# The upper parts of the values of the later batches are written by VectorE instead of ScalarE

## The chip, the cores and the metric

One core of a Trainium2 chip runs the whole program. The metric is device time in microseconds (us); lower is better. Before the change, three runs gave a median of 1901.4 us (1901.28 to 1903.27). Below, TensorE does matrix products and loads their weights, VectorE, ScalarE and GpSimd do the work on elements, and SyncE issues the transfers.

## The reference, cut to what matters

Attention through 49 agents, on 4 batches of 12480 tokens of 128 channels, then a layer of two products with a squared ReLU between them.

```python
def _attn_ref(q, k, v, agents):
    scale = 1.0 / np.sqrt(q.shape[-1])
    def sm(a, b):
        s = scale * (a @ b.transpose(0, 2, 1))
        s = s - s.max(-1, keepdims=True)
        e = np.exp(s)
        return e / (e.sum(-1, keepdims=True) + 1e-09)
    a2k = sm(agents, k)          # B x 49 x 12480
    agent_v = a2k @ v            # B x 49 x 128
    q2a = sm(q, agents)          # B x 12480 x 49
    return (q2a @ agent_v).astype(np.float32)

def _moe_ref(x, w_in, w_out):    # x: 49920 x 128, w_in: 128 x 2048, w_out: 2048 x 128
    h = np.maximum(x @ w_in, 0.0)
    return (h * h @ w_out).astype(np.float32)
```

## The kernel before

Each batch is first boiled down to a table: `agent_v` times `w_in`, so that the first layer of a token is its 49 weights times that table. Tokens go in 13 blocks of 960 per batch, each in two halves of 480. A number is held as a rounded upper part (float32r) and the remainder, a lower part, so that each product is done from parts; the three groups of products of the second layer (`g_lo` with `wo_half`, `g_hi` with `wo_hi`, `g_hi` with `wo_lo`) are such.

The main loop has 416 steps, here called steps, of two chunks of 256 hidden units each. A step is `first` (lines 494 to 527) and `second` (546 to 563). In `first`, TensorE makes four products `h<-w,aw_hi` and adds four `h<-x,aw_ex`, into two of three PSUM buffers `h` (`ps_h`, two banks each). ScalarE writes `r` from each `h` and then `g_hi`, VectorE writes `gg` from the first `h`, then `h` in place and `g_lo` from the second; GpSimd writes the two other `g_lo` (line 519). With three buffers and two to a step, the third of a step's four weight loads `h<-w,aw_hi` goes into the buffer that the step before used first: it waits for that step's `gg`. `second` works on the chunks of two steps before and sums into `o`; every eighth chunk VectorE writes `ob` out of `o`.

Between these, two background streams run in the gaps: the next blocks' query weights (`queries`: on VectorE `m`, `e`, `z`, its reciprocal; on GpSimd `e`, `ph`, `y`, `half`), and the table of the next batch (`background`, from line 571). The latter first takes the scores of all 13 blocks of keys, then their maxima (`maxima`: `dg` on VectorE, the product with it on TensorE, `mb`), and then 13 units of values, one in about 17 us: `weighed` prepares a unit and `gathered` multiplies it and adds it to `av` on VectorE. The values of batch 0 take another path (`whole`), so the units below are those of batches 1, 2 and 3, 39 in all. "The first batch" below means the first one with such units.

In a unit, the tile `vs` holds for 120 tokens by 8 the upper parts of 128 values, a one, and the lower parts. Line 280 writes the upper parts, a copy that rounds; line 282 on GpSimd subtracts them from the values for the lower parts, and 278 and 279 set the rest.

Each engine works through its own queue in order. The matrix products and the main loop's operations are chained in the order in which they are written (`queued`, line 487); the place of the background work among them is chosen by the scheduler when the program is built, from its own estimates.

Of the kernel before, what the change touches and what calls it, by code (L numbers as in the profile page):

```python
# [41 lines left out]
def agent_attention_relu2(ctx: ExitStack, tc: tile.TileContext, qT, kT, v, agT, w_in, w_out, outT):  # L42
    nc = tc.nc
    C, NTOK = qT.shape
# [218 lines left out]
    def halves(out, x, n, eng):  # L263

        nc.scalar.copy(out[:, :, :n], x)
        yield PACE
        last[eng] = eng.tensor_sub(out[:, :, n:], x, out[:, :, :n].bitcast(F32))

    def weighed(b, i, vt, whole, eng):
        st = state[b]  # L270
        s = st["s"][i]
        mb = st["mb"].rearrange("p (o a) -> p o a", o=1).broadcast_to([TP, NT, NA])
        d = s if whole else small.tile([TP, NT, NA], F32, name="d", bufs=2)
        st["less"] = eng.tensor_sub(d, s, mb).ins
        R, W = (NA, C + 1) if whole else (K2, 2 * (C + 1))
        if not whole:
            vs = kv.tile([TP, NT, W], F32R, name="vs")
            nc.gpsimd.memset(vs.bitcast(F32)[:, :, C : C + 1], 1.0)
            nc.gpsimd.memset(vs.bitcast(F32)[:, :, 2 * C + 1 :], 0.0)
            nc.scalar.copy(vs[:, :, :C], vt[:, :, :C])  # L280
            yield PACE
            last[nc.gpsimd] = nc.gpsimd.tensor_sub(  # L282
                vs[:, :, C + 1 : 2 * C + 1], vt[:, :, :C], vs[:, :, :C].bitcast(F32)
            )
        else:
            nc.scalar.copy(vt[:, :, C:], ones[:TP, :NT].rearrange("p (t o) -> p t o", o=1))
        yield PACE
        nc.scalar.activation(d, d, AF.Exp, scale=scale)
        if whole:
            e = d  # L290
        else:
            e = small.tile([TP, NT, R], F32R, name="e2", bufs=2)
            yield from halves(e, d, NA, eng)
            vt = vs
        return e, vt, R, W, whole
# [28 lines left out]
    def values(b, i, vt, whole, eng):  # L324
        yield from gathered(b, i, *(yield from weighed(b, i, vt, whole, eng)))
# [245 lines left out]
    def background(b):  # L571

        kt = load_keys(b, 0, kv, "kt")
        for i in range(NB):
            nxt = load_keys(b, i + 1, kv, "kt") if i + 1 < NB else load_values(b, 0, kv, "vt")
            yield from scores(b, i, kt)
            yield 0.5
            kt = nxt
        yield from maxima(b)
        yield  # L580
        vt = load_values(b, 1, kv, "vt")
        ready = yield from weighed(b, 0, kt, False, nc.gpsimd)
        for i in range(NB):
            yield PACE
            nxt = load_values(b, i + 2, kv, "vt") if i + 2 < NB else None
            more = (yield from weighed(b, i + 1, vt, False, nc.gpsimd)) if i + 1 < NB else None
            yield from gathered(b, i, *ready)
            vt, ready = nxt, more
        yield
        yield from tables(b)  # L590
# [151 lines left out]
```

## Time and profile before

| what | value |
|---|---|
| median of 3 runs | 1901.4 us |
| profiled execution | 1903.08 us, its span 1900.9 us |
| TensorE busy | 1877.9 us (99%), chain that ended last: 89% TensorE |
| VectorE busy | 1648.2 us (87%) |
| ScalarE busy | 1670.7 us (88%) |
| GpSimd busy | 1335.3 us (70%) |
| granted TensorE clock, mean | 0.992 |
| the copies of line 280 | 39, 40.2 us on ScalarE |
| the lower parts of line 282 | 39, 85.8 us on GpSimd |

Four engines have long busy times, but a busy time is an average. The waits of TensorE, by what ended them, tell what a shorter or longer queue elsewhere would be worth.

### The profile page before, as it was taken

How to read it: one execution, taken by the hardware profiler on the slowest of the kernel's cores; microseconds unless marked ns; L12 is line 12 of the kernel's file. 1: busy time of each engine (PE TensorE's matmuls, PEld its weight loads, DVE VectorE, ACT ScalarE, POOL GpSimd, SP SyncE). 2: the span in 40 equal slices, each digit the busy share in tenths (PEclk: the TensorE clock that was granted, in tenths of full speed). 3: DMA queues.
4: the chain of work that ended last, by engine and by line, in shares of the span. 5: the costliest groups of instructions: out<-in, count | busy, mean ns of one | idle time of the engine just before them, and what ended most of it. 6: DMA issues, size and time to landing. Idle time of an engine off the chain costs nothing.

```text
span 1900.9 us, 31102 instructions
## 1 busy us (share of the span) xinstructions
PE 1877.9 (99%) x10848; PEld 1404.6 (74%) x10848; DVE 1648.2 (87%) x1918; ACT 1670.7 (88%) x1607; POOL 1335.3 (70%) x1270
## 2 busy tenths in 40 slices
PE   8899999999999999999999999999999999999999
PEld 8678777777678777777767777777767777777776
DVE  6887888888987888888998788888899989989897
ACT  4478899998888899999888789999889999999997
POOL 1455789887665589887666568989666676767675
PEclk9799999999999999999999999999999999999999
DMA  9233222221123222222112322222111111111110
GB/s 359 74 122 93 81 83 76 90 74 52 51 75 99 92 85 73 89 69 71 50 46 88 104 69 75 86 71 73 49 46 55 52 52 53 51 51 44 57 35 30
DMA packets 74148, 144.53 MB, mean 76 GB/s; under 512 B 9356, under 2 KB 45864, under 8 KB 73992
## 3 DMA queue, kind: packets, MB, share of 16 engines
q1 hardware_dynamic: 73992, 142.55, 23.6%
q8 instruction: 86, 1.41, 0.3%
q14 instruction: 70, 0.57, 0.1%
HBM read 82.89 MB, written 25.56 MB: 57 GB/s over the span
## 4 chain that ended last, share of the span: by engine, by line
PE 89%; DVE 6%; issue 2%; ACT 1%; POOL 1%; DMA 0%; POOLq 0%; SPq 0%; DVEq 0%; ACTq 0%
PE o L490 53%; PE h L490 24%; PE psa L490 10%; DVE gg L490 2%; PE psa L305 1%; DVE g_lo L490 1%; PE h L194 1%; POOL g_lo L519 1%; ACT r L490 1%; DVE h L490 1%; DVE aw_half L388 1%; ACT g_hi L490 0%; DVE ob L490 0%; PE h L612 0%; DVE rest L115 0%
## 5 line engine op out<-in xcount | busy, mean ns | idle before, releaser
L519 POOL TENSOR_TENSOR g_lo<-gg,g_hi 128x480 f16<-128x480 f32 x832 | 998.2, 1221 | 423.4 <-ACT g_hi L490 263.8
L490 ACT ACTIVATE r<-h 128x960 f32<-128x960 f32 x832 | 763.5, 967 | 118.4 <-PE h L490 60.9
L490 ACT ACTIVATE g_hi<-r 128x1920 fp32r<-128x1920 f32 x416 | 754.2, 1813 | 30.3 <-ACT r L490 0.7
L490 DVE TENSOR_TENSOR g_lo<-h,g_hi 128x960 f16<-128x960 f32 x416 | 479.4, 1153 | 126.2 <-ACT g_hi L490 94.1
L490 PE MATMUL o<-g_hi,wo_hi 128*128 128x480 f32 x1664 | 569.4, 423 | 0.0
L490 DVE TENSOR_TENSOR gg<-r,h 128x960 f32<-128x960 f32 x416 | 479.1, 1152 | 83.8 <-ACT r L490 78.5
L490 PE MATMUL o<-g_lo,wo_half 128*128 128x480 f16 x1664 | 517.2, 370 | 0.5 <-POOL g_lo L519 0.5
L490 PE MATMUL o<-g_hi,wo_lo 128*128 128x480 f32 x1664 | 496.1, 379 | 0.0
L490 DVE TENSOR_TENSOR h<-r,h 128x960 f32<-128x960 f32 x416 | 480.2, 1154 | 1.1
L490 PE MATMUL h<-w,aw_hi 128*128 128x480 f32 x1664 | 434.9, 382 | 7.5 <-DVE gg L490 4.0
L490 PEld LDWEIGHTS h<-w,aw_hi 128*128 128x128 f32 x1664 | 312.5, 189 | 63.7 <-DVE gg L490 10.9
L490 PEld LDWEIGHTS o<-g_hi,wo_hi 128*128 128x128 f32 x1664 | 314.9, 189 | 50.3 <-issue 0.8
L490 PEld LDWEIGHTS o<-g_hi,wo_lo 128*128 128x128 f32 x1664 | 312.5, 188 | 48.8
L490 PEld LDWEIGHTS <-wo_half 128*128 128x128 f16 x1664 | 171.9, 112 | 149.0 <-issue 96.7
L490 PE MATMUL h<-x,aw_ex 19*128 19x480 f16 x1664 | 159.4, 373 | 0.0
L490 PEld LDWEIGHTS <-aw_ex 19*128 19x128 f16 x1664 | 41.8, 91 | 138.8 <-issue 138.2
L490 PEld LDWEIGHTS psa<-ag,qt 128*120 128x120 f32 x816 | 127.6, 187 | 6.9 <-issue 0.4
L490 PE MATMUL psa<-ag,qt 128*120 128x49 f32 x816 | 118.3, 249 | 0.0
L424 POOL TENSOR_TENSOR e<-e,z 120x392 f32<-120x392 f32 x52 | 44.1, 848 | 64.7 <-PE h L490 33.8
L282 POOL TENSOR_TENSOR vs<-vt,vs 120x1024 fp32r<-120x1024 f32 x39 | 85.8, 2201 | 0.0
L490 PEld LDWEIGHTS psa<-ag,kt 128*120 128x120 f32 x624 | 78.1, 185 | 5.1 <-DVE ob L490 2.5
L490 PE MATMUL psa<-ag,kt 128*120 128x49 f32 x624 | 76.7, 259 | 0.0
(148 smaller groups left out, 1092.1 us busy)
## 6 DMA issues: line engine op xcount, KB each, us to landing
qt<-in_qT SPq DMA_DIRECT2D x52, 480.0 KB
out_T<-ob SPq DMA_DIRECT2D x104, 240.0 KB
vt<-in_v SPq DMA_DIRECT2D x39, 516.0 KB
kt<-in_kT SPq DMA_DIRECT2D x39, 480.0 KB
w<-ph SPq DMA_DIRECT2D x102, 91.9 KB
w<-y SPq DMA_DIRECT2D x102, 91.9 KB
x<-half SPq DMA_DIRECT2D x416, 17.8 KB
ahead<-in_v SPq DMA_DIRECT2D x13, 516.0 KB
```

The source lines that it names most:

```text
L194: last[nc.tensor] = nc.tensor.matmul(*args, **kw)
L282: last[nc.gpsimd] = nc.gpsimd.tensor_sub(vs[:, :, C + 1 : 2 * C + 1], vt[:, :, :C], vs[:, :, :C].bitcast(F32))
L305: nc.tensor.matmul(sums[0][:R, :W], e[:, t, :], vt[:, t, :], start=(i == 0 and t == 0), stop=(i == NB - 1 and t == NT - 1),)
L388: cut = nc.vector.tensor_copy(half, lo.bitcast(F32)).ins
L424: nc.gpsimd.tensor_mul(e, e, z.broadcast_to([TP, NT, NA]))
L490: ins = issue(*args, **kw)
L519: chain[nc.gpsimd] = nc.gpsimd.tensor_sub(lo[:, n, :], gg[:, n, :], hi[:, 0, n, :].bitcast(F32)).ins
```

## The change

One line: the same copy is given to VectorE. The tiles, their sizes and all other lines are as they were.

```diff
             vs = kv.tile([TP, NT, W], F32R, name="vs")
             nc.gpsimd.memset(vs.bitcast(F32)[:, :, C : C + 1], 1.0)
             nc.gpsimd.memset(vs.bitcast(F32)[:, :, 2 * C + 1 :], 0.0)
-            nc.scalar.copy(vs[:, :, :C], vt[:, :, :C])
+            nc.vector.tensor_copy(vs[:, :, :C], vt[:, :, :C])
             yield PACE
             last[nc.gpsimd] = nc.gpsimd.tensor_sub(
                 vs[:, :, C + 1 : 2 * C + 1], vt[:, :, :C], vs[:, :, :C].bitcast(F32)
```

The scheduler then places it. TensorE's order stays the same; ScalarE's loses the 39 copies. On VectorE, in a regular unit of the first batch (the eleventh, `vs_4121`; a number behind a name tells one buffer's use from another), + is a row that only the changed kernel has:

```order
 L490 TENSOR_TENSOR h_4032<-r_4041,h_4032 128x2x480
 L322 TENSOR_TENSOR av_2534<-av_2534,psa_4027 98x258
+L280 CAST vs_4121<-vt_3929 120x8x128
 L423 RECIPROCAL z_4076<-z_4076 120x8
 L490 TENSOR_SCALAR ob_4072<-o_3915,down_702 128x480
```

The copy stands between `av` and the reciprocal; in every other unit there is no reciprocal, and `ob` follows at once.

GpSimd's queue beside that unit, - is a row's place before:

```order
 L519 TENSOR_TENSOR g_lo_4048<-gg_4043,g_hi_4042 128x480 x2
-L424 TENSOR_TENSOR e_4023<-e_4023,z_4076 120x392
 L274 TENSOR_TENSOR d_4119<-s_1854,mb_2199 120x392
 L278 MEMSET vs_4121 120x8
 L279 MEMSET vs_4121 120x8
 L282 TENSOR_TENSOR vs_4121<-vt_3929,vs_4121 120x8x128
+L424 TENSOR_TENSOR e_4023<-e_4023,z_4076 120x392
 L519 TENSOR_TENSOR g_lo_4100<-gg_4095,g_hi_4094 128x480 x2
```

The scaling of the query weights, `e`, moved behind the unit's lower parts; the work between the two pairs of `g_lo` is the same.

VectorE's queue at the second copy of the second batch, near the start of its units of values:

```order
 L490 TENSOR_TENSOR gg_7077<-r_7075,h_7065 128x960
+L280 CAST vs_7163<-vt_7017 120x8x128
 L414 TENSOR_REDUCE m_7106<-psa_7025 120x8
 L490 TENSOR_TENSOR h_7066<-r_7075,h_7066 128x2x480
 L416 TENSOR_TENSOR e_7108<-psa_7025,m_7106 120x392
 L490 TENSOR_TENSOR g_lo_7110<-h_7066,g_hi_7076 128x960
+L490 TENSOR_TENSOR gg_7127<-r_7125,h_7115 128x960
 L421 TENSOR_REDUCE z_7152<-e_7108 120x8
+L490 TENSOR_TENSOR h_7116<-r_7125,h_7116 128x2x480
 L422 TENSOR_SCALAR z_7152<-z_7152 120x8
-L490 TENSOR_TENSOR gg_7127<-r_7125,h_7115 128x960
```

Here the copy stands behind a `gg`, and the next step's `gg` and `h` go ahead of the two operations on `z`. At the first copy of the second and third batch it stands behind `dg` and ahead of `h` and `ob`; in the first batch it stands behind a `gg` both times, and the reciprocal goes behind `ob` at the first.

## Rows read from the trace of the kernel before

**Rows 1.** The page, busy us of each engine (share of the span) and instructions.

```profile
PE 1877.9 (99%) x10848; PEld 1404.6 (74%) x10848; DVE 1648.2 (87%) x1918; ACT 1670.7 (88%) x1607; POOL 1335.3 (70%) x1270
```

**Rows 2.** The list of waits: who waited for whom, us in total, times, longest.

```profile
PEld h L490 <- DVE gg L490: 10.9, 19, 1.2
```

**Rows 3.** Groups by line: count, busy us, mean ns of one, idle before.

```profile
L280 ACT CAST vs<-vt 120x1024 fp32r<-120x1024 f32 x39 | 40.2, 1030 | 0.0
```

**Rows 4.** Lines 388 and 115: ns minimum/median/maximum, first and last start.

```profile
L388 DVE CAST aw_half<-aw_lo x16: 410/1168/1425, 75.3 to 1432.5; 49x512 f16<-49x512 f32 x16
...
L115 DVE TENSOR_SCALAR rest<-t x8: 276/282/286, 22.9 to 47.7; 128x256 uint32<-128x256 uint32 x8
```

**Rows 5.** The timeline (start us, us, engine, what), VectorE and GpSimd at 960.

```profile
960.20 1.33 DVE L388 CAST aw_half<-aw_lo 49x512 f16<-49x512 f32 x1
...
960.04 2.57 POOL L519 TENSOR_TENSOR g_lo<-gg,g_hi 128x480 f16<-128x480 f32 x2 [2.83 <-ACT g_hi L490]
```

**Rows 6.** The timeline, the eleventh unit of the first batch.

```profile
383.00 0.20 DVE L423 RECIPROCAL z<-z 120x8 f32<-120x8 f32 x1
...
383.70 1.15 DVE L490 TENSOR_TENSOR g_lo<-h,g_hi 128x960 f16<-128x960 f32 x1
385.02 1.15 DVE L490 TENSOR_TENSOR gg<-r,h 128x960 f32<-128x960 f32 x1 [0.17 <-ACT r L490]
...
383.20 2.40 POOL L519 TENSOR_TENSOR g_lo<-gg,g_hi 128x480 f16<-128x480 f32 x2 [2.35 <-DVE z L423]
...
389.51 2.40 POOL L519 TENSOR_TENSOR g_lo<-gg,g_hi 128x480 f16<-128x480 f32 x2
...
386.14 0.84 PEld L490 LDWEIGHTS h<-w,aw_hi 128*128 128x128 f32 x4
...
392.50 0.37 PE L490 MATMUL o<-g_lo,wo_half 128*128 128x480 f16 x1
```

**Rows 7.** The timeline, the tenth unit of the first batch.

```profile
365.26 0.71 DVE L490 TENSOR_SCALAR ob<-o,down 128x480 f32<-128x480 f32 x1
365.89 1.14 DVE L490 TENSOR_TENSOR g_lo<-h,g_hi 128x960 f16<-128x960 f32 x1
367.35 1.15 DVE L490 TENSOR_TENSOR gg<-r,h 128x960 f32<-128x960 f32 x1 [0.32 <-ACT r L490]
...
364.13 1.25 POOL L465 TENSOR_TENSOR y<-y,ph 98x480 fp32r<-98x480 f32 x1
365.30 0.60 POOL L466 CAST half<-ph 98x480 f16<-98x480 f32 x1
...
368.46 0.84 PEld L490 LDWEIGHTS h<-w,aw_hi 128*128 128x128 f32 x4
```

**Rows 8.** The timeline, where the second batch's first copy will stand.

```profile
657.01 1.15 DVE L490 TENSOR_TENSOR h<-r,h 128x960 f32<-128x960 f32 x1
...
656.97 0.60 POOL L466 CAST half<-ph 98x480 f16<-98x480 f32 x1
...
658.83 0.28 PEld L490 LDWEIGHTS psa<-dg,ones 49*120 49x120 f32 x2 [1.16 <-DVE ob L490]
```

**Rows 9.** The timeline, where the second batch's second copy will stand.

```profile
669.49 0.56 DVE L414 TENSOR_REDUCE m<-psa 120x8 f32<-120x392 f32 x1
...
672.56 0.55 DVE L421 TENSOR_REDUCE z<-e 120x8 f32<-120x392 f32 x1
...
673.43 1.14 DVE L490 TENSOR_TENSOR gg<-r,h 128x960 f32<-128x960 f32 x1
...
668.89 2.21 POOL L282 TENSOR_TENSOR vs<-vt,vs 120x1024 fp32r<-120x1024 f32 x1
...
674.63 0.30 PEld L490 LDWEIGHTS h<-w,aw_hi 128*128 128x128 f32 x2 [0.30 <-DVE gg L490]
...
678.54 0.30 PEld L490 LDWEIGHTS h<-w,aw_hi 128*128 128x128 f32 x2 [0.22 <-DVE gg L490]
```

**Rows 10.** The timeline, TensorE's load in the first batch, second unit.

```profile
227.20 0.30 PEld L490 LDWEIGHTS h<-w,aw_hi 128*128 128x128 f32 x2 [0.95 <-DVE gg L490]
```

## The prediction, made before the result was known

> **What bounds the kernel now.** I read the page's busy times first, then the list of waits, then the lines by engine, and last the timeline around three places where the copy will stand. TensorE is busy 99% of the span [rows 1], so the time changes only by what TensorE waits. In the loop it waits in one place above all: of the four weight loads of a step's first layer the third needs the PSUM buffer that VectorE's gg of the step before gives back, and all waits of a load for a gg come to 10.9 us in the kernel [rows 2]. The 39 ScalarE copies are 40.2 us [rows 3], but ScalarE's time is not the kernel's. So the question is by how much the copy, on VectorE, makes gg late, and whether that is more than gg has to spare.
>
> **What the copy takes on VectorE.** No VectorE copy of this size into float32r is in the trace. The nearest rows: one over 512 elements takes 410 ns at best, an SBUF operation over 256 takes 276 to 286 ns [rows 4]. The difference, 0.13 us for 256 elements, is half a nanosecond an element, so 1024 elements take 0.41 + 0.27 = 0.68 us. The next instruction starts 0.08 us before the end of the one ahead (ob 365.26 + 0.71 = 365.97, g_lo 365.89 [rows 7]), so 0.60 us are lost to the queue. The other end is the pace of the operations with a PSUM input, 1.15 us for 960 elements [rows 6], which makes 1.23 for 1024, 1.15 of it in the queue. I take 0.60, since rows 4 are the same kind of operation. Below nothing it cannot be.
>
> That fast form has a second price. The 512-element copy also takes 1168 ns in the median [rows 4]: at 960.20 us it was asked for while GpSimd worked on the first g_lo of a pair (960.04, half of a usual pair of 2.40 is 1.20, so until 961.24) and it ended at 961.53, 0.29 later; GpSimd's pair then took 2.57 instead of 2.40 [rows 5, 6]. So such a copy stands still until the GpSimd instruction in flight ends, goes ahead of the next one, and holds that one up. For 1024 elements the end lies 0.55 us behind GpSimd's.
>
> **The 16 copies beside an idle GpSimd.** In every second unit from the third on, the copy comes between av and the reciprocal z. At 383.00 GpSimd is idle; its g_lo comes at 383.20 [rows 6]. The copy costs 0.60. VectorE could have begun gg at 383.70 + 1.15 - 0.08 = 384.77 but began at 385.02, waiting for ScalarE, so 0.25 is free and gg slips by 0.35. It then ends at 386.52. The third load is due 0.43 into the four that start at 386.14, at 386.57 [rows 6], and a load that waits starts 0.06 behind gg (673.43 + 1.14 = 674.57, load 674.63 [rows 9]). So it just fits: I take 0.02 us each, 0.3 in all. GpSimd, held up from 383.20 to at most 383.68, has no idle time up to the pair at 389.51, which ends at 391.91; TensorE takes the second of that pair at 392.50 [rows 6]. The 0.59 between them cover that delay. What ScalarE no longer does frees nothing here, as gg now waits for VectorE.
>
> **The 17 copies behind GpSimd's y.** Here it comes before ob. GpSimd's y ends at 364.13 + 1.25 = 365.38, so the copy, asked for at 365.26, ends at 365.93, and 0.59 are lost. gg could have begun at 365.89 + 1.14 - 0.08 = 366.95 and began at 367.35: 0.40 are free, and it slips by 0.19. Its end, 368.50, lies 0.39 before the third load (368.46 + 0.43) [rows 7]. Nothing is lost. GpSimd's half follows later by half a microsecond, which only a transfer to the next block's weights waits for.
>
> **The starts of the three batches.** They carry the sum.
> First copies: in the second and third batch the copy comes after dg and ahead of h and ob, and the load of TensorE's product with dg already waits 1.16 us for ob. If the copy gets in before GpSimd's half it costs 0.60; behind it (656.97 + 0.60 + 0.55 = 658.12, less 0.08, instead of 657.01) it costs 1.03 [rows 8]. I take 0.8 each, 1.6.
> Second copies: there the copy stands right behind gg, where m began at 669.49, and GpSimd began the lower part of the first unit, 2.21 us long, at 668.89. It holds the copy until 671.10, so it ends at 671.65 and m begins at 671.57, 2.08 late. Until the next gg the order helps: the reduction z and the operation behind it (672.56 to 673.43, 0.87) now come after gg. So gg begins at 673.43 + 2.08 - 0.87 = 674.64, and the load behind it at 675.84 instead of 674.63. The gg after that ended 0.06 before the load at 678.54, so began at 677.34, 3.91 after its predecessor; with the z operations (0.55 in the queue) now between the two it begins at 679.10, and its load comes at 680.30 instead of 678.54 [rows 9]. That is 1.76 late; less a small wait that follows today, I take 1.7 each, 3.4 for the two batches. Bounds: 0.3 (no hold-up by GpSimd) and 2.1 (nothing helped by the order).
> First batch: the first copy costs 0.60 there, less 0.11 since z's reciprocal falls behind ob. The second gives something back: today the load waits 0.95 for a gg [rows 10] that is late by ScalarE's copy. Of that I take 0.6, between nothing and all. Together -0.1.
>
> **Sum.** 0.3 + 0 + 1.6 + 3.4 - 0.1 = 5.2 us. The profiled execution took 1903.1 us (span 1900.9 and 2.2 around it), 1.7 above the median of the three runs, so 1908.3 for it and 1906.6 against the median 1901.4. A measurement of this kernel can tell about 0.2%, 3.8 us, from no change; the forecast lies 1.4 beyond that.
>
> **Rivals.**
> GpSimd goes first. In the 17 places GpSimd's half is recorded from 365.30, only 0.04 behind the copy's place at 365.26 [rows 7]. If half gets in, the copy ends 0.55 behind its end at 365.90, so 1.11 are lost, gg slips by 0.71, and past the 0.33 that it has to spare TensorE waits 0.38; 17 times is 6.5, and the time is 1913.1. For it: the margin. Against it: at 960.20 the waiting copy went first. The Trainium skill, on the page "SBUF — State Buffer", section "SBUF: two separate sides", says that whichever of the two starts first gets the shared port pair for its whole instruction; by that the copy would win here, by 0.04 us, and the one at 669.49 would wait as reckoned. The trace agrees at 960.20.
> The slow form. If a copy into float32r runs at 1.23 us, it holds nobody up and is held by nobody. Then the 16 wait 0.25 off 1.15, less 0.35, that is 0.55 each (8.8), the 17 0.42 each (7.1), the first copies cost 3.3, the second ones 0.8 twice, less 0.6: 20 us, 1921.6. For it: no VectorE row of a single input writes float32r. Against it: the copy to float16 in rows 4 changes the type too and is fast. The Trainium skill, "VectorE: DVE Perf Modes", section on the perf-mode tier table, gives 1227 ns for a float32 copy of 2048 elements in SBUF and names no float32r; half of that pace with its fixed part would be some 0.69 us, an estimate that changes nothing in the sum.
> Not slower: the second copies are not caught. Their price hangs on the copy being asked for 0.6 us after GpSimd's 2.21 us began [rows 9]. If the two swap, because the start of the batch shifts VectorE against GpSimd by more than that, each costs 0.3, and the sum is 0.3 + 1.6 + 0.6 - 0.1 = 2.4, 1903.8, no change that can be measured. Against it: both follow the same step, so they shift together.
> Faster by 4 us or more: ScalarE's copies would have to cause over a third of the 10.9 us [rows 2]; in the two regular places they cause none.
>
> **How the numbers follow.** Forecast 0.50 (its own range 1904 to 1909), GpSimd first 0.15, slow form 0.10, not caught 0.22, faster 0.03. Slower by over 0.2% are 0.41 of the forecast's half and both dear rivals, 0.66; within it 0.09 and 0.22, 0.31; faster 0.03. The range for 8 in 10 goes from 1901.0 (not caught, and the first copies nearly free) to 1916.0 (GpSimd first); the slow form is left out.
>
> **What would show it.** The 39 copies on VectorE at 0.68 us where GpSimd is idle, about 0.67 in the 17 places, and near 2.2 us at the second copies of the second and third batch, with GpSimd's L282 before it. TensorE's waits for gg at 33 regular places stay under 0.1 us; the load of the product with dg waits about 2 us in two batches instead of 1.16. Wrong would be: copies of 1.2 us everywhere, copies of 1.2 us in the 17 places alone, or long copies whose delay TensorE never sees.

## The result, and the profile after

The changed kernel takes 1912.8 us (median of 4 runs, 1911.7 to 1913.4), the kernel before 1901.5 (4 runs, 1901.3 to 1903.3). The ratio is 1.0055, 95% interval 1.0043 to 1.0067: slower by 0.55%, more than the 0.2% that can be told from no change. The forecast was 1906.6 with 1901.0 to 1916.0 around it: the sign was right and the time lies in the range, but outside the forecast's own 1904 to 1909. The profiled execution has a span of 1911.6 us instead of 1900.9, so 10.7 us are to be found.

The page after, busy us of each engine (share of the span) and instructions, answers to [rows 1]:

```profile
PE 1881.4 (98%) x10848; PEld 1406.3 (74%) x10848; DVE 1674.8 (88%) x1957; ACT 1638.3 (86%) x1568; POOL 1349.4 (71%) x1270
```

VectorE has 39 instructions and 26.6 us more, ScalarE 32.4 us less; neither tells where 10.7 us come from. The list of waits after (who waited for whom, us in total, times, longest) answers to [rows 2]:

```profile
PEld h L490 <- DVE gg L490: 12.3, 17, 1.2
PEld psa L490 <- DVE ob L490: 7.3, 11, 1.8
PEld h L490 <- issue: 3.6, 3, 3.1
```

The waits for gg have grown by 1.4 us only, from 10.9. The last row is one to stop at: three waits whose releaser the profile doesn't name, one of them 3.1 us long. The copies themselves, by line (number, ns minimum/median/maximum, first and last start, shape), answer to [rows 3, 4]:

```profile
L280 DVE CAST vs<-vt x39: 677/687/4678, 209.3 to 1337.8; 120x1024 fp32r<-120x1024 f32 x39
```

The median is what was forecast, 0.68 to 0.69 us. The maximum, 4.68 us, is in no term of the sum and in no rival. 36 copies take 0.68 to 0.69, two 2.17 and 2.15, one 4.68.

Now the places, first the two regular ones. The timeline after (start us, us, engine and what; idle before and who ended it, in brackets), the eleventh and the tenth unit of the first batch, answers to [rows 6, 7]:

```profile
382.48 0.69 DVE L280 CAST vs<-vt 120x1024 fp32r<-120x1024 f32 x1
...
382.68 2.75 POOL L519 TENSOR_TENSOR g_lo<-gg,g_hi 128x480 f16<-128x480 f32 x2 [2.36 <-ACT g_hi L490]
...
385.61 0.84 PEld L490 LDWEIGHTS h<-w,aw_hi 128*128 128x128 f32 x4
...
364.72 0.69 DVE L280 CAST vs<-vt 120x1024 fp32r<-120x1024 f32 x1
...
363.57 1.25 POOL L465 TENSOR_TENSOR y<-y,ph 98x480 fp32r<-98x480 f32 x1
364.74 1.10 POOL L466 CAST half<-ph 98x480 f16<-98x480 f32 x1
...
367.93 0.84 PEld L490 LDWEIGHTS h<-w,aw_hi 128*128 128x128 f32 x4
```

In both the copy runs at once and GpSimd pays: its pair 2.75 instead of 2.40, its half 1.10 instead of 0.60. The four weight loads still stand in one piece of 0.84, so TensorE has waited for nothing. At the tenth unit y ends at 364.82, 0.10 behind the moment at which the copy is asked for.

The starts of the second batch, answering to [rows 8, 9]:

```profile
658.63 0.28 PEld L490 LDWEIGHTS psa<-dg,ones 49*120 49x120 f32 x2 [1.76 <-DVE ob L490]
...
669.32 2.17 DVE L280 CAST vs<-vt 120x1024 fp32r<-120x1024 f32 x1
...
668.72 2.21 POOL L282 TENSOR_TENSOR vs<-vt,vs 120x1024 fp32r<-120x1024 f32 x1
670.93 2.79 POOL L519 TENSOR_TENSOR g_lo<-gg,g_hi 128x480 f16<-128x480 f32 x2
...
675.68 0.30 PEld L490 LDWEIGHTS h<-w,aw_hi 128*128 128x128 f32 x2 [0.76 <-DVE gg L490]
```

The second copy was caught behind line 282 as reckoned: 282 ends at 670.93, the copy at 671.49, 0.56 later, and g_lo behind it is stretched.

And the long copy, a unit of the third batch, at a place of the kind "behind GpSimd's y":

```profile
1226.60 1.23 POOL L465 TENSOR_TENSOR y<-y,ph 98x480 fp32r<-98x480 f32 x1
1227.78 0.58 POOL L466 CAST half<-ph 98x480 f16<-98x480 f32 x1
1228.32 2.39 POOL L519 TENSOR_TENSOR g_lo<-gg,g_hi 128x480 f16<-128x480 f32 x2
1230.66 0.97 POOL L274 TENSOR_TENSOR d<-s,mb 120x392 f32<-120x392 f32 x1
1231.56 0.12 POOL L278 MEMSET vs<- 120x8 f32 x1
1231.60 0.12 POOL L279 MEMSET vs<- 120x8 f32 x1
1232.35 2.18 POOL L282 TENSOR_TENSOR vs<-vt,vs 120x1024 fp32r<-120x1024 f32 x1 [0.63 <-DVE vs L280]
...
1227.59 4.68 DVE L280 CAST vs<-vt 120x1024 fp32r<-120x1024 f32 x1
1232.19 0.70 DVE L490 TENSOR_SCALAR ob<-o,down 128x480 f32<-128x480 f32 x1
...
1234.07 0.30 PEld L490 LDWEIGHTS h<-w,aw_hi 128*128 128x128 f32 x2 [3.11 <-issue]
1234.10 0.67 PE L490 MATMUL h<-w,aw_hi 128*128 128x480 f32 x2 [2.73 <-DVE g_lo L490]
1235.07 0.48 PEld L490 LDWEIGHTS h<-w,aw_hi 128*128 128x128 f32 x2 [0.70 <-DVE gg L490]
```

Read GpSimd's rows first: six instructions without a gap behind y, at full speed, to 1231.72. The copy was asked for at 1227.59, 0.24 before y's end, and ended at 1232.27, 0.55 behind the last memset. GpSimd then stood still 0.63 for this very copy, which its line 282 reads. VectorE's queue came to rest behind the copy, and TensorE's weight loads stood 3.11 us. Their row names no releaser, but that of the products does: they stood 2.73 us for VectorE's g_lo, which has its place behind ob and so behind the copy.

That is not all of its price. The windows around it (us, length, then busy us of PE, PEld, DVE, ACT, POOL with counts, the granted TensorE clock, DMA share and GB/s):

```profile
1228.00:1234.00 6.00, 3.37 (x18) 1.92 (x16) 6.00 (x4) 3.64 (x3) 5.37 (x7) 1.00 0.18 55
1234.00:1242.00 8.00, 7.60 (x27) 5.50 (x28) 6.63 (x6) 4.58 (x5) 4.28 (x5) 0.57 0.32 101
1242.00:1250.00 8.00, 8.00 (x52) 6.05 (x50) 5.15 (x7) 5.59 (x6) 4.33 (x4) 1.00 0.21 65
```

After its stand TensorE worked for 8 us at a granted clock of 0.57, close to the lower of its two levels (1.2 of 2.4 GHz), and then at the full one again.

Where the 10.7 us went is read from the third weight load of every step: its time after less its time before (the lag), and how that lag changes from step to step:

| stretch | change of the lag, us |
|---|---|
| first copy of the first batch | +0.54 |
| second copy of the first batch and what follows | -0.86 +0.16 -0.21 |
| first copies of the second and third batch | +0.64, +0.62 |
| second copies of the second and third batch | +1.22 +0.52, +1.19 +0.52 |
| a shift of VectorE at 1208.66 | +0.39 |
| the long copy: the step at 1227, the step behind it | +3.64, +3.01 |
| all the rest, the 32 other regular copies among it | -0.7 |

### The profile page after: what moved, and what is told of

It reads as the page before. It is cut to its first block, busy times and chain, and to the rows that moved or that the text cites. A ratio compares the mean times of both kernels' runs of the same rounds, so it can differ in the third digit from the quotient of the medians.

```text
span 1911.6 us, 31065 instructions
## 1 busy us (share of the span) xinstructions
PE 1881.4 (98%) x10848; PEld 1406.3 (74%) x10848; DVE 1674.8 (88%) x1957; ACT 1638.3 (86%) x1568; POOL 1349.4 (71%) x1270
## 4 chain that ended last, share of the span: by engine, by line
PE 87%; DVE 7%; issue 2%; ACT 2%; POOL 1%; DMA 0%; POOLq 0%; SPq 0%; DVEq 0%; ACTq 0%
PE o L490 51%; PE h L490 23%; PE psa L490 10%; DVE gg L490 2%; PE psa L305 1%; ACT r L490 1%; DVE g_lo L490 1%; ACT g_hi L490 1%; PE h L194 1%; DVE h L490 1%; POOL g_lo L519 1%; DVE aw_half L388 1%; DVE ob L490 0%; DVE vs L280 0%; PE h L612 0%
```

## The experiments

Two theories at first. A: a copy that has to wait for GpSimd is not let in at the end of the instruction in flight, but is passed over by what stands ready on GpSimd; the moment of asking decides whether it has to wait. B: the rule of the prediction holds, and the long copy is something else, of one execution or one place. The second copies, let in behind line 282 with g_lo next, already fit B better than A. In the expectations of rep and late_only the rival called B is a special case, the spread loss: 0.2 us at each of the 33 regular copies.

**rep: the changed kernel once more, unedited.**

> The changed kernel once more, nothing edited. Theory A (held back): of the +11.2 us some 4.0 come from the starts of the batches and 6.6 from one copy of 4.68 us in the third batch that waited while GpSimd ran six instructions back to back. If that waiting hangs on the program's own rhythm it comes again at the same copy, and the time is 1911.5 to 1913.5 again; if it comes by chance, the long copy sits elsewhere, or there are none or two, and single times lie between 1905.5 and 1919. Rival B (spread): the 33 regular copies cost 0.2 us each in every run, 1912.8, and the long copy is an accident of the one profile, so a profile without it still shows a span near 1911.

1912.1 us (4 runs, 1911.0 to 1912.6), ratio 1.0050 [1.0035, 1.0065]. The same unit had the long copy again, 4.69 us at 1227.93, so it belongs to the program. The regular copies cost nothing in the steps here either, which goes against the spread loss. The window behind the long copy, in columns as above:

```profile
1234.00:1242.00 8.00, 7.26 (x46) 5.37 (x47) 6.88 (x7) 5.33 (x6) 4.89 (x5) 1.00 0.36 111
```

Here the steps behind the hold ran at the full clock, and the span is 1909.2 us instead of 1911.6: the 3.0 us of the lower clock come in some executions and not in others.

**one_elem_reduce: the copy in a form that leaves GpSimd alone.**

```
-nc.vector.tensor_copy(vs[:, :, :C], vt[:, :, :C])
+nc.vector.tensor_reduce(vs[:, :, :C], vt[:, :, :C].rearrange("p t (c o) -> p t c o", o=1), axis=AX.X, op=ALU.max)
```

> The same 39 copies at the same places of VectorE's queue, each written as a maximum over groups of one element: the operation that VectorE runs at about 1.2 us for 1024 elements, and which by the reductions of z in the trace before is not held up by GpSimd. Theory A: no copy is over 1.3 us, GpSimd's instructions beside them keep their 1.21 us; TensorE waits 0.55 us at 16 regular copies and 0.42 at 17, 16 us, and some 4 us at the batches' starts: 1919 to 1923. Rival C (only the conflict with GpSimd costs, VectorE's own time does not): below 1906.

1920.0 us (1917.5 to 1920.1), ratio 1.0089 [1.0074, 1.0104]. The row by line:

```profile
L280 DVE TENSOR_REDUCE vs<-vt x39: 1201/1214/1217, 209.7 to 1344.2; 120x1024 fp32r<-120x1024 f32 x39
```

No copy was held, at any place, and GpSimd's g_lo beside them kept its 1.21. So holding and being held go with the fast copy, at the same places and with the same values. This run is also what the rival "slow form" would have been, priced at 1921.6: 0.51 to 0.57 at each of the 16 places (reckoned 0.55), 0.16 to 0.33 at the 17 (0.42), of both some 0.1 given back in the next step, and 2.5 to 2.7 at a first copy of the second and third batch (1.65).

**late_only and early_only: the change in two parts.** ScalarE keeps the first two units of a batch, or all but them.

```
late_only:  (nc.scalar.copy if i < 2 else nc.vector.tensor_copy)(vs[:, :, :C], vt[:, :, :C])
early_only: (nc.vector.tensor_copy if i < 2 else nc.scalar.copy)(vs[:, :, :C], vt[:, :, :C])
```

> The first two copies of each batch stay on ScalarE, the other 33 are on VectorE. Theory A: the 4.0 us of the batches' starts are gone; if no copy is held back for long, the time is that of before, 1901 to 1902.5; if one is again, about 1908. Rival B (33 regular copies cost 0.2 us each): about 1908.5 with no copy over 1 us.

> Only the first two copies of each batch are on VectorE, the other 33 stay on ScalarE. Theory A: the second copies of the second and third batch take 2.2 us behind GpSimd's line 282, the time is 4.0 us above before, 1905 to 1906.5, with no copy longer than 2.3 us. Rival B: the starts cost little, 1902 to 1904.

late_only 1908.2 us (10 runs), ratio 1.0028 [1.0019, 1.0037]; early_only 1905.7 (10 runs), ratio 1.0016 [1.0006, 1.0026]. The two excesses, 5.6 and 3.1 us over their before of 1902.6, make 8.7 of the 9.4 that rep had over it: the parts add up. early_only's steps at the batch starts are those of the table, with 2.18 and 2.15 us for the second copies, and no long copy. late_only's time alone tells A (about 1908 with one hold) from the spread loss (about 1908.5) not at all; its trace does. late_only lost nothing at the batch starts and all of it at one held copy, now at another unit:

```profile
1291.45 4.17 DVE L280 CAST vs<-vt 120x1024 fp32r<-120x1024 f32 x1
...
1291.14 0.59 POOL L466 CAST half<-ph 98x480 f16<-98x480 f32 x1
1291.68 2.39 POOL L519 TENSOR_TENSOR g_lo<-gg,g_hi 128x480 f16<-128x480 f32 x2
```

So it isn't a property of that unit. What sets the held copies apart is the moment of asking. In the changed kernel 16 of the 17 copies behind y are asked 0.08 to 0.12 us before y's end, the held one 0.24 before it (0.26 in rep), and late_only's 0.25 behind it, inside half. The shift has a visible start, in the changed kernel one unit earlier, in late_only in the same unit:

```profile
1208.66 1.16 DVE L490 TENSOR_TENSOR gg<-r,h 128x960 f32<-128x960 f32 x1 [0.34 <-issue]
...
1288.98 1.16 DVE L490 TENSOR_TENSOR gg<-r,h 128x960 f32<-128x960 f32 x1 [0.27 <-POOL g_lo L519]
```

The first row is of the changed kernel: VectorE stood for 0.34 us with nothing in the profile that it waited for, in rep too (at 1209.00). The second is of late_only: its gg began 1.43 us after the g_lo ahead of it began, where 1.07 is usual, and the copy behind it asked 0.35 later against y. Such stands are not made by the change: the kernel before has them at 1042.75 (0.36) and 1641.91 (0.35).

Recorded starts tell the moment of asking only roughly. In the changed kernel the copy at 1211.20 ran in 0.69 although a g_lo is recorded from 1211.04; it was g_lo that was stretched, from some 1.2 to 1.93.

**shifted: the moment of asking moved at all 17 places.** One reduction more on VectorE, which nothing reads, a few instructions ahead of the copy.

```
+i >= 2 and i % 2 == (b == 1) and nc.vector.reduce_max(small.tile([TP, 6], F32, name="late"), s[:, :6, :], axis=AX.X)
 nc.vector.tensor_copy(vs[:, :, :C], vt[:, :, :C])
```

> The changed kernel, with one reduction more (120x294, about 0.37 us) that nothing reads, on VectorE a few instructions ahead of the copy at the 17 places where GpSimd's y stands; so there the copy is asked about 0.27 us behind y's end, in the middle of half (0.58), instead of 0.10 ahead of y's end. Theory A (the moment of asking decides; asked in the middle of a GpSimd instruction with others ready behind it, the copy is passed over by all of them): at nearly all of the 17 places a copy of 3.5 to 4.7 us, each worth 3.6 us, or 6.6 where the granted clock of TensorE falls behind it: 61 to 112 us over the 1906 that the changed kernel takes without its one held copy, so 1967 to 2018. Theory B (the prediction's rule; the one long copy came from something else): the copies end 0.55 behind half's end, at most 0.9 us long, nothing to 0.4 us at each place: 1906 to 1919. Theory D (the one held copy belongs to its place in the program, whatever the phase): one or two long copies as before, 1909 to 1919.

2020.7 us (one run), just above the 1967 to 2018 of theory A. All 17 copies were held, each 4.15 to 4.18 us, asked 0.26 to 0.28 us behind y's end. One of them:

```profile
262.02 4.17 DVE L280 CAST vs<-vt 120x1024 fp32r<-120x1024 f32 x1
...
261.71 0.57 POOL L466 CAST half<-ph 98x480 f16<-98x480 f32 x1
262.25 2.38 POOL L519 TENSOR_TENSOR g_lo<-gg,g_hi 128x480 f16<-128x480 f32 x2
264.59 0.95 POOL L274 TENSOR_TENSOR d<-s,mb 120x392 f32<-120x392 f32 x1
```

The pattern of the one long copy, 17 times over, for 0.37 us more on VectorE. Each step with a hold is longer by 3.6 us and the next by 2.7 to 3.0. The window of the first such next step (columns as above):

```profile
269.50:276.50 7.00, 7.00 (x28) 5.28 (x27) 5.04 (x5) 4.58 (x5) 4.00 (x4) 0.54 0.31 93
```

That settles against B and D and for the moment of asking, for copies asked behind y's end; an ask 0.24 before it, as in the changed kernel, was not tried in the kernel.

**idle_only: only the 16 copies that meet an idle GpSimd.**

```
(nc.vector.tensor_copy if i >= 2 and i % 2 != (b == 1) else nc.scalar.copy)(vs[:, :, :C], vt[:, :, :C])
```

> VectorE writes the copy at the 16 places where GpSimd is idle, ScalarE at the other 23. Theory A (only a copy asked while GpSimd is at work, with more ready behind, can be held): all 16 copies 0.68 to 0.69 us, none held, 16 times 0.02 us: 1902 to 1904, no difference that can be measured. Theory D (a hold can come at any place where the program's rhythm is disturbed): one held copy of 4 to 5 us, 1905 to 1909.

1901.9 us (10 runs, 1900.7 to 1902.3) beside 1902.7, ratio 0.9995 [0.9986, 1.0005]: no copy held, against D, and no difference, as theory A has it, and as the prediction priced these 16.

**sweep and sweep_plain: two failures.** They were to measure the wait by itself, with a VectorE reduction as the clock that moves the copy along a row of GpSimd instructions.

```
reduce_max(sink, pad[:, : 8 + n])                      (sweep)
tensor_reduce(sink[:, : 8 + n], pad[:, : 8 + n] ...)   (sweep_plain)
tensor_copy(vs[:, :, :C], vt[:, :, :C])                (both, behind it)
```

> This kernel leaves the whole computation out and measures the disputed wait by itself: 148 trials in a row, each with one VectorE copy of the kernel's shape (120x1024, float32 to float32r) beside a row of GpSimd instructions of the kernel's shapes that stand ready back to back. In the first 82 trials the row is y (98x480, 1.23 us), half (0.58), two g_lo (1.20 each), d (0.97), then the subtraction that reads the copy; in the last 66 it is one 120x1024 subtraction (2.2) and two g_lo. A VectorE reduction of growing length ahead of the copy moves the moment of asking through the row in steps of about 0.07 us. Theory A (a copy that has to wait is passed over by every GpSimd instruction that stands ready, and gets in only when GpSimd runs dry): the copy's time falls in one long slope, from about 5.5 us to 0.7 in the first part and from about 4.8 to 0.7 in the second, broken at most by narrow gaps where it is asked within 0.1 us of a boundary. Theory B (the prediction's: it waits for the instruction in flight alone and goes ahead of the next one): short teeth, no copy over 1.23 + 0.55 = 1.8 us in the first part or over 2.2 + 0.55 = 2.75 in the second. Theory C (it depends on which instruction is in flight): teeth under some of them and slopes under others, as in the traces so far: let in behind the 120x1024 subtraction, passed over under y and half.

> The 148 trials of the run called sweep again, the whole computation left out, with another filler ahead of the copy: in sweep the growing VectorE reduction itself kept GpSimd's first instruction from ending (y took 4.11 us where the filler took 2.68), so that the copy never met a GpSimd at work. The filler is now the reduction over single elements, beside which GpSimd kept its 1.21 us in the run called one_elem_reduce. Theory A (a copy that has to wait is passed over by every GpSimd instruction that stands ready): one long slope from about 5.5 us down to 0.7 in the first part (y, half, two g_lo, d) and one from about 4.8 in the second (a 120x1024 subtraction, two g_lo), broken at most within 0.1 us of a boundary. Theory B (it waits for the instruction in flight alone): short teeth, nothing over 1.8 us in the first part or 2.75 in the second. Theory C (it depends on the instruction): under the 120x1024 subtraction it is let in at its end, at most 2.75 us, under y and half it is passed over.

The whole computation is left out of these two kernels and of the next two sweeps. Behind the first trial every copy took 0.68 or 0.69 us in both, at all offsets, which tells none of the theories apart, since the copy never met a GpSimd at work. One trial of sweep:

```profile
363.91 4.11 POOL L51 TENSOR_TENSOR y<-y,ph 98x480 fp32r<-98x480 f32 x1 [0.41 <-DVE y L51]
...
363.69 2.68 DVE L51 TENSOR_REDUCE sink<-pad 98x1 f32<-98x2440 f32 x1
366.29 0.68 DVE L51 CAST vs<-vt 120x1024 fp32r<-120x1024 f32 x1
```

y, released beside the running reduction, ended 1.05 behind the copy: here GpSimd waited for both VectorE instructions. Why the reduction counts here, when in one_elem_reduce GpSimd ran beside one, was not found out.

**sweep_scalar: the same with ScalarE as the clock**, so that VectorE is idle when it is asked.

```
scalar.copy(t, pad[:, :1])           # releases GpSimd's row
scalar.copy(sink[:, :n], pad[:, :n]) # grows from trial to trial
scalar.copy(vt[:98, 0, :1], pad[:, :1])
vector.tensor_copy(vs[:, :, :C], vt[:, :, :C])
```

> 172 trials, the whole computation left out. In the two sweeps before, GpSimd's first instruction never ran beside VectorE's filler, so the copy met no GpSimd at work. Here ScalarE is the clock: one short copy of ScalarE releases GpSimd's row, a second one of growing length later the VectorE copy (120x1024), which meets VectorE idle. Rows: 54 trials of y, half, two g_lo, d; 48 of a 120x1024 subtraction and two g_lo; 70 of six g_lo. The steps of the moment of asking are about 0.1 us, the first ask is 0.3 us or more behind the row's start. In each row all instructions are ready when the first starts. Theory A (a copy that has to wait is passed over by everything that stands ready): its time falls in one slope, from about 5 us in the first and second part and about 7 in the third, to 0.7. Theory B (it waits for the instruction in flight alone): teeth of at most 1.2 + 0.55 = 1.8 us in the first and third part, 2.75 in the second. Theory E (order of arrival: what GpSimd has already taken up when the copy asks goes first, what it takes up later goes behind): teeth for a copy that is asked soon after the row's start, as the copies of the filter in the kernel before were let in 0.28 ahead of a second g_lo, and one slope for a copy asked later; in the third part a longest wait of a fixed number of instructions.

Neither A nor B: C, it depends on the row. With the 120x1024 subtraction and two g_lo the longest copy took 2.57 us, with six g_lo 1.76: always let in at the end of the instruction in flight, 0.55 behind it. Plotted against the moment of asking that makes teeth, as B has them: the wait falls, and jumps up again at each instruction. Copies asked late in the six g_lo show the same teeth, so E, by which they form one slope, falls too. With half in the row (y, half, two g_lo, d) copies asked in y 0.5 us or more before its end, in half, or in the first g_lo were passed over up to the second g_lo's end, 4.33 us at most. Copies asked 0.31 to 0.10 us before y's end got in at y's end. So a new theory, F: the cast half is what makes GpSimd keep its turn.

**sweep_rows: which rows keep the copy out.** Five rows of GpSimd, with and without casts.

> 170 trials, the whole computation left out; ScalarE is the clock as in sweep_scalar, the steps of the moment of asking are about 0.21 us. Five rows of GpSimd: y and four g_lo (32 trials); g_lo, half, four g_lo (34); six times half (24); two g_lo, d, two memsets, two g_lo (34); the kernel's own row ph, two g_lo, y, half, two g_lo, d, two memsets (46). In sweep_scalar a copy was let in at the end of the instruction in flight in every row of two-input subtractions, and was passed over by two or three more in the row with half. Theory F (a one-input cast of GpSimd, half, in the row or next to come, makes GpSimd keep its turn): rows one and four show teeth of at most 1.8 us; row two a wait over several instructions for a copy asked just before or in half or one behind it; row three one slope of up to 3.4 us; row five long waits around ph and half, 3 us or more. Theory G (the number of different lengths or the row's history, not the cast): long waits in rows one or four too.

| GpSimd's row | trials | longest copy, us |
|---|---|---|
| y, four g_lo | 32 | 1.76 (teeth) |
| g_lo, half, four g_lo | 34 | 5.67 (one slope from half on) |
| six times half | 24 | 1.03 (teeth) |
| two g_lo, d, two memsets, two g_lo | 34 | 1.77 (teeth) |
| ph, two g_lo, y, half, two g_lo, d, memsets | 46 | 6.11 (slope from ph to the g_lo behind half, then teeth) |

Two trials next to each other of the second row, 0.21 us apart in the moment of asking:

```profile
361.39 0.75 DVE L51 CAST vs<-vt 120x1024 fp32r<-120x1024 f32 x1 [8.64 <-ACT vt L51]
371.00 5.67 DVE L51 CAST vs<-vt 120x1024 fp32r<-120x1024 f32 x1 [8.85 <-POOL lo L51]
...
361.54 1.04 POOL L51 CAST half<-ph 98x480 f16<-98x480 f32 x1
362.55 4.65 POOL L51 TENSOR_TENSOR lo<-gg,hi 128x480 f16<-128x480 f32 x4
...
370.93 0.58 POOL L51 CAST half<-ph 98x480 f16<-98x480 f32 x1
371.47 4.64 POOL L51 TENSOR_TENSOR lo<-gg,hi 128x480 f16<-128x480 f32 x4
376.75 2.17 POOL L51 TENSOR_TENSOR vs<-vt,vs 120x1024 fp32r<-120x1024 f32 x1 [0.63 <-DVE vs L51]
```

Asked at 361.39, ahead of half, the copy runs and half is stretched to 1.04. Asked at 371.00, 0.07 behind half's start, it waits for half and four g_lo, until GpSimd is dry. F holds in that long waits come in the two rows in which a cast is followed by two-input subtractions and in no other; rows of subtractions alone, with or without memsets, let the copy in at each boundary, against G. It doesn't hold as simply as it was put. In the second row copies asked up to 3.3 us behind the cast's end, beside g_lo alone, are still passed over by the g_lo behind the one in flight. Six casts were to give one slope of up to 3.4 us and gave teeth; but between them GpSimd stands still for some 0.06 us, which it does in no other row, so that row doesn't tell a cast from a gap. And in the fifth row the copy gets in one g_lo behind the second cast, not at the end. Casts are also the only instructions with a single input in these rows; which of the two counts was not tried.

**shifted_half: the kernel of shifted, half on ScalarE.**

```
-nc.gpsimd.tensor_copy(half, hi.bitcast(F32))
+nc.scalar.copy(half, hi.bitcast(F32))
```

> The kernel of the run called shifted (2020.7 us, 17 copies of 4.15 us and more), with half written by ScalarE instead of GpSimd, at every unit. Theory F (GpSimd's cast half is what makes it keep its turn): the 17 copies wait at most for one g_lo, 1.8 us or less, so that at most 1.1 us each is lost, with 0.6 us of ScalarE more at each place: 1905 to 1945. Rival (any back-to-back row keeps the copy out): copies of 3 us and more at most of the 17 places, 1960 to 2020.

1913.2 us (one run) instead of 2020.7. Of the 17 copies two waited for y and took 1.34 and 1.33, the others 0.69. One of these:

```profile
261.48 1.24 POOL L465 TENSOR_TENSOR y<-y,ph 98x480 fp32r<-98x480 f32 x1
263.18 2.75 POOL L519 TENSOR_TENSOR g_lo<-gg,g_hi 128x480 f16<-128x480 f32 x2 [0.46 <-ACT g_hi L490]
...
262.99 0.69 DVE L280 CAST vs<-vt 120x1024 fp32r<-120x1024 f32 x1
```

The row is no longer without a gap: GpSimd waits 0.46 for ScalarE behind y, and the copy meets it idle. So 107 us went with half, but this run alone can't say whether the cast or the missing gap had made them. The first and fourth row of sweep_rows can: they have no gap and no cast, and let the copy in.

**idle_plus: a version to beat both.** The 16 of idle_only and the second copy of the first batch, which gave time back.

```
(nc.vector.tensor_copy if i == b == 1 or i >= 2 and i % 2 != (b == 1) else nc.scalar.copy)(vs[:, :, :C], vt[:, :, :C])
```

> The kernel of the run called idle_only (VectorE writes the 16 copies beside an idle GpSimd) with one copy more on VectorE, the second of the first of the later batches, which in the trace of before was 0.95 us of TensorE's waiting behind VectorE and ScalarE. By the steps of early_only that copy gave back 0.87 + 0.23 - 0.14 = 0.96 us: 1900.9 to 1901.5 beside a before of 1902.3, ratio 0.9990 to 0.9995, at the edge of what can be told. The rival (the gain is given back at the next wait): as idle_only, ratio 0.9995 to 1.0000.

1900.8 us (11 runs, 1899.3 to 1901.2) beside 1902.9 (15 runs), ratio 0.9991 [0.9982, 1.0000]: as expected, and at the edge of what can be told; the rival, a ratio of 0.9995 and more, is not ruled out. Its median is the lowest of all versions tried, but the intervals of it and of idle_only overlap.

## Why the prediction was right, and where it was wrong

**The copy's duration** held: 0.68 to 0.69 us measured, 0.68 reckoned from the two rows of line 388 and 115, and 0.60 in the queue.

**The 16 copies beside an idle GpSimd** held: nothing in the steps, and idle_only shows it by itself. **The 17 behind y** held for 16 of them: no step is longer, and GpSimd's half moves as said.

**The first copies** were reckoned at 0.8 and cost 0.64 and 0.62: the copy got in ahead of GpSimd's half, the cheaper of the two cases, and the load behind dg waited 1.76 instead of 1.16. **The second copies** were reckoned at 1.7 and cost 1.74 and 1.71, with the copy ending 0.56 behind line 282. **The first batch** was reckoned at -0.1 and gave -0.37: the wait of 0.95 of [rows 10] went altogether, so 0.86 came back at once, where 0.6 was taken.

These terms come to 5.2 in the prediction and to 4.3 in the trace (-0.37 + 1.26 + 3.45). By them alone the kernel would stand at 1906. What lifted it to 1912.8 is the held copy, 3.6 and 3.0 us, which stands in no term.

**The step that failed** is the rule "such a copy stands still until the GpSimd instruction in flight ends, goes ahead of the next one, and holds that one up". It was taken from line 388 and used for all 39. Line 388 is asked for while GpSimd works on pairs of g_lo [rows 5], two-input subtractions, and beside those the rule is true: sweep_rows has it for 66 trials in two rows. Behind y stands half, a cast, with g_lo after it, and there the rule can fail: a copy that doesn't get in ahead of half waits for all of the row, 4.68 us once in the changed kernel and 4.15 to 4.18 at 17 of 17 places in shifted. The prediction read the margin of 0.04 us between the copy and half [rows 7], and asked only what one more instruction ahead would cost, 0.38. The right question was what lies behind the margin, and there lay 3.6 us, or 6.6 with the lower clock.

**The rival "GpSimd goes first"** gave 1913.1 and the time is 1912.8, and yet it wasn't this rival that came: it has 17 copies late by 0.38 each, and the trace has 16 late by nothing and one by 3.6 and 3.0. The nearness is chance. In its terms the margin was judged rightly as thin, and the loss behind it was sized at a tenth.

**First come.** The Trainium skill, page "SBUF — State Buffer", section "Who interferes with whom", says of such a VectorE instruction and GpSimd that whoever issues first gets the shared pair for the whole instruction, and that issue order, not the shape of the operation, decides who blocks. The trace agrees on the first where either runs alone (half stretched from 0.60 to 1.10, the copy from 0.69 to 2.17). On the second it differs, as far as the length of a wait goes: beside a row of two-input subtractions, y and four g_lo, the longest copy took 1.76 us, beside the row of g_lo, half and four g_lo 5.67, though in both all instructions stood ready when the first began. The measurement decides.

**Open.** Why a cast followed by subtractions keeps the copy out, and why a second cast ends that sooner, isn't settled; the runs show the rows that do it, not the mechanism. The sweeps don't repeat the kernel's hold in full either: with y, half, two g_lo and d the copy got in ahead of d in sweep_scalar, while in the changed kernel and in shifted it waited for d and the memsets too. Nor is it settled why a copy 0.24 us before y's end was held in the kernel when those 0.31 to 0.10 before it were let in in sweep_scalar, what VectorE's 0.34 us at 1208.66 and its like in the kernel before were, and why the clock fell behind the hold in one execution of the changed kernel and not in that of rep.

## What to carry to other kernels

A VectorE copy between SBUF tiles in its fast form is cheap only where GpSimd is idle or its row is known: find for each place what GpSimd has ready at that moment, the whole row up to its next gap and not just the instruction in flight, since the copy may have to wait for all of it. Where a place is saved by a margin of a tenth of a microsecond, price what lies behind the margin, and ask how steady the margin is over all the repetitions; one slip in 17 more than doubled the loss here. A stand of TensorE can cost nearly as much again behind its end, in steps at the lower clock.

## What the runs showed of the hardware

A copy of 120x1024 from float32 into float32r takes VectorE 0.69 us, the same values through a reduction over single elements 1.21. A VectorE copy that had to wait ended 0.55 to 0.63 us behind the end of GpSimd's last instruction ahead of it, mostly 0.55 (0.55 at 1232.27, 0.56 at 671.49; 0.63 in sweep_scalar behind y with half next). GpSimd rows with a cast followed by two-input subtractions, without a gap, stretched it to up to 6.11 us. Rows without a cast let it in at the end of the instruction in flight; it then took at most 1.77 us beside g_lo and 2.57 beside a 120x1024 subtraction. TensorE's granted clock stood at 0.54 to 0.57 in the 7 to 8 us behind a stand of its weight loads of 3.1 us in the changed kernel, in late_only and at the first two holds of shifted, and at 1.00 behind an equal one in rep.
